# A new written-out command order, with other engines for copies and masks, in a fused attention and maxout-FFN kernel

## The chip, the cores and the metric

The kernel runs on one core of one Trainium2 chip. The metric is device time in microseconds (us). Before the change six runs gave a median of 193.53 us (192.91 to 194.72).

The core's engines work side by side, each through its own queue in order: PE (TensorE: matmuls and transposes through the array), DVE (VectorE), ACT (ScalarE), POOL (GpSimd) and SP (SyncE, which here only issues transfers). An instruction that waits holds up everything behind it on its engine; semaphores tie the engines to one another.

## The reference, cut to what matters

```python
# q, k, v: (batch 4, heads 8, seq 768, head_dim 64)
scores = scale * q @ k.T                       # per batch and head
keep   = causal                                # retrieval heads (0, 2, 6)
keep   = causal & (first 4 keys | last 64)     # streaming heads (the others)
a      = softmax(where(keep, scores, -1e9))
x      = (a @ v), heads side by side           # (3072 tokens, 512)
h      = max(x @ w1, x @ w2, x @ w3)           # (3072, 768)
out    = h @ w_out                             # (3072, 512), float32
```

## The kernel before, in words

**Tiling.** The sequence of each of the four batches is cut into two halves of 384 tokens (three blocks of 128). A step `t` of the attention is a batch, a half and one of two groups of four heads: `t = 4*batch + 2*half + group`, 16 in all, and each step is worked as two pairs of heads (`i` = 0 or 1). The FFN (line 570) is worked per half batch, so eight times; it needs the attention output of all four head pairs of that half (steps `4*batch + 2*half` and the next one).

**The order is written by hand.** The whole kernel is the list of strings `PROGRAM` (line 132). `run` (line 895) reads it from the first command to the last and calls one small function for each. The scheduler is told to keep that order (`tc.manual_schedule()`), so a command's place in the list is its place in the queue of each engine that it uses. The commands, with the line of the function:

- `ld`, `load`, `load_v`, `load_vp`, `w` (279, 350, 406, 552): transfers from HBM. `ld`, `load`, `load_vp` and `w` (the four weight matrices, converted to half precision on the way) are issued by POOL, `load_v` by SP. The first q and k are loaded ahead of the program by SP and ACT.
- `cast`, `turnp` (310, 322): for batch 0, conversion of k and q to half precision, and transposes through PE, copied out of PSUM (line 341). The last letters name the engines: `d` DVE, `a` ACT, `p` POOL; `cast 0 0 pd` casts k on POOL and q on DVE.
- `turn b g i part` (380): for batches 1 to 3, a quarter of the transposes of one group of heads, on DVE (line 388).
- `um`, `o` (531, 363): mask tables, and the copies of the first keys into places where streaming heads find them.
- `s t u [i]` (690): score matmuls of unit `u` of step `t` into the PSUM tiles `st` (two buffers, each holds one pair of heads), and their exponentials on ACT (line 748).
- `k t i u e` (754): multiplies the exponentials by 0/1 masks, on DVE or POOL, one to three instructions (lines 762, 782, 797).
- `v t i ee` (651): v to half precision (line 656, the first letter), and copies for the streaming heads (lines 660 to 672, the second letter).
- `av t i` (801): products with v into a PSUM bank, then the reciprocal of the sums and the scaling, both on DVE (lines 831, 834).
- `x t i e` (840): transposes the scaled output for the FFN. `D` is one transposing transfer issued by SP (line 847); `a` and `d` are three transposes on PE and a copy on ACT or DVE (lines 853, 854).
- `f 1 e` (641): one step of the FFN that is at the head of a queue. Of the 24 steps of one FFN, 18 are products: four matmuls of 128x384 (line 591) into a PSUM bank; a third of them are then copied out by ACT or DVE, as `e` says (line 608), the others go through a maximum on DVE always (line 611). In the first two stages (batch 0) the six products with w1 come first, then w2's, then w3's; later the three alternate. The other six are three output steps (six matmuls of 128x512, line 627, a copy by ACT or DVE at line 633, a transfer by SP at line 634), each followed by an empty one.
- `gate`, `pad` (400, 397): transfers of a few bytes on SP.

There are four PSUM banks for everything but the scores (`bkp`, line 253): products, outputs, `av` and transposes share them. A buffer that is asked for again waits for whoever still reads it: three each for v (`vs`), for the transposed q and k (`KQ`), for each xT and for the output tile (`ot`).

The idea of the order is that the FFN steps of one half batch fill PE while the other engines work on the attention of the next one. Below, "step n of the FFN stage" counts the `f` commands, 192 in all: stage 0 is f 1 to 24, stage 1 is f 25 to 48, and so on.

The four lines in which the output's transposes and the FFN meet:

```python
if op is None:                                   # D
    nc.sync.dma_start(out=xt, in_=..., transpose=True)
...
if hp == NHP - 1:
    queue.append(ffn(b, half))
```

Of the kernel before, what the change touches and what calls it, by code (L numbers as in the profile page):

```python
# [129 lines left out]
)  # L130

PROGRAM = (
    "cast 0 0 ad, load_v 0 0, cast 0 1 pp, ld 1 0, um 1 1, turnp 0 1 aa, um 1 0, cast 0 3 pa",
    "um 0 1, s 0 0 1, s 0 1 1 b, turnp 0 3 a, cast 0 2 pp, ld 1 2, turnp 0 0 ad, turnp 0 2 ad",
    "um 0 0, cast 1 1 dd, s 0 0 0, cast 1 0 dd, w 0, s 1 0 0, s 0 1 0 b, load_vp 0 1, o 0 0 0 p",
    "v 0 1 dd, v 1 1 dd, v 0 0 dp, turnp 1 0 d, turnp 1 1 da, s 1 0 1, av 0 0, w 1, av 0 1",
    "o 0 1 0 p, cast 1 2 pa, s 1 1 1, s 1 1 0 b, s 2 0 1, v 1 0 pp, cast 1 3 ap, av 1 1",
    "s 2 0 0, av 1 0, x 1 0 d, x 0 0 a, turnp 1 2 dd, s 2 1, x 0 1 d, w 2, x 1 1 d, turnp 1 3 d",
    "f 1 d, s 3 0, k 2 0 1 d, f 1 d, k 3 0 0 d, w 3, o 0 0 1 p, s 3 1 0, k 3 1 0 d, f 1 a",
    "f 1 d, o 0 1 1 d, k 2 1 1 d, s 2 2, v 3 0 dp, f 1 d, k 3 0 1 d, load 1 0, f 1 d, k 2 0 2 d",  # L140
    "v 2 1 dd, s 2 3, av 3 0, s 3 1 1, f 1 a, f 1 d, f 1 d, k 2 1 3 p, v 3 1 ap, k 2 0 3 d",
    "f 1 d, av 2 1, k 3 1 1 p, f 1 a, f 1 d, gate, f 1 d, f 1 d, v 2 0 ad, f 1 a, av 3 1, f 1 d",
    "av 2 0, f 1 a, f 1 d, load 1 1, x 2 0 a, x 3 0 a, f 1 a, load_v 1 0, load 2 0",
    "turn 1 0 0 0, f 1 d, turn 1 0 0 1, x 2 1 a, turn 1 0 1 0, x 3 1 a, f 1 a, f 1 d, f 1 a",
    "turn 1 0 1 1, turn 1 1 0 1, f 1 a, f 1 a, f 1 a, f 1 a, f 1 a, turn 1 1 0 0, f 1 a",
    "turn 1 1 1 1, f 1 a, turn 1 1 1 0, f 1 d, turn 2 0 0 0, load_v 1 1, s 5 0, k 5 0 0 p",
    "f 1 a, load 2 1, f 1 d, f 1 d, s 4 0, turn 2 0 1 1, f 1 a, k 4 0 0 d, f 1 d, f 1 d, s 5 1",
    "o 1 0 0 d, f 1 d, f 1 a, k 4 1 0 d, s 4 1, k 5 1 0 d, o 1 1 0 p, v 5 0 pp, f 1 a, s 5 2",
    "v 4 0 dp, k 4 0 1 d, f 1 a, k 4 1 1 d, k 5 0 2 d, f 1 d, av 4 0, v 4 1 pd, v 5 1 ap",
    "turn 2 0 0 1, s 6 0, f 1 a, k 5 1 2 p, av 5 0, v 6 0 dd, av 4 1, s 6 1, x 4 0 D, f 1 a",  # L150
    "k 6 0 1 p, av 5 1, turn 2 0 1 0, x 5 0 D, k 5 0 1 d, x 4 1 D, k 6 1 1 p, f 1 a, f 1 d",
    "v 7 1 pp, s 6 2, k 6 0 2 d, x 5 1 a, f 1 a, v 7 0 pp, f 1 a, s 6 3, turn 2 1 1 1",
    "turn 2 1 1 0, f 1 a, v 6 1 pd, f 1 a, k 6 1 3 p, f 1 d, turn 2 1 0 1, f 1 a, turn 2 1 0 0",
    "f 1 d, f 1 a, f 1 a, av 6 1, k 5 1 1 p, s 8 0, f 1 d, av 7 0, load_v 2 0, f 1 a, load 3 1",
    "pad, k 6 0 3 d, av 7 1, s 9 0, x 6 1 D, f 1 d, f 1 d, v 9 1 pp, f 1 a, v 9 0 dp, f 1 a",
    "v 8 1 dd, s 9 1, f 1 a, turn 3 1 1 1, av 6 0, load 3 0, o 2 0 0 d, x 6 0 D, turn 3 1 0 0",
    "f 1 a, x 7 0 D, x 7 1 D, s 8 1, f 1 a, f 1 d, s 10 0, o 2 1 0 p, f 1 d, k 8 0 1 d, f 1 a",
    "turn 3 1 1 0, load_v 2 1, s 9 2, k 9 0 2 d, k 9 1 2 d, f 1 a, f 1 a, v 8 0 ap, f 1 d",
    "f 1 a, k 8 0 0 p, k 9 0 0 d, turn 3 1 0 1, v 10 0 pd, v 11 1 pp, f 1 d, f 1 a, load_v 3 0",
    "f 1 d, f 1 d, f 1 a, k 8 1 0 d, k 9 1 0 d, s 10 1, av 9 0, f 1 a, av 8 0, f 1 a, f 1 a",  # L160
    "v 11 0 pd, f 1 d, f 1 d, k 8 1 1 d, f 1 a, v 12 0 dp, k 9 1 1 p, s 10 2, x 8 0 D, av 9 1",
    "f 1 d, f 1 a, f 1 a, s 10 3, turn 3 0 0 0, av 8 1, x 9 0 D, f 1 a, f 1 d, x 8 1 D, f 1 a",
    "f 1 d, k 10 0 1 p, f 1 d, turn 3 0 0 1, x 9 1 D, k 10 0 3 d, k 10 0 2 d, turn 3 0 1 0",
    "f 1 a, f 1 d, f 1 d, load_v 3 1, f 1 a, k 9 0 1 d, av 10 0, f 1 a, k 10 1 3 p, f 1 d",
    "f 1 d, v 12 1 pp, f 1 a, turn 3 0 1 1, av 11 0, k 10 1 1 p, f 1 d, f 1 a, f 1 a, s 13 0",
    "v 13 1 pp, f 1 d, av 11 1, f 1 d, f 1 a, x 10 0 D, x 11 0 D, v 10 1 ap, v 15 1 pd, s 12 0",
    "f 1 a, f 1 d, f 1 a, f 1 d, f 1 a, k 13 1 0 d, s 13 1, o 3 1 0 p, f 1 a, av 10 1, s 12 1",
    "k 13 0 0 d, f 1 d, f 1 a, s 14 0, k 12 1 1 p, x 10 1 D, f 1 d, x 11 1 D, f 1 a, f 1 d",
    "k 12 0 0 d, f 1 a, f 1 d, k 12 1 0 d, f 1 a, f 1 a, k 13 0 1 d, f 1 d, v 14 1 dd",
    "o 3 0 0 p, s 13 2, k 13 1 1 d, f 1 d, f 1 d, f 1 d, k 13 1 2 p, av 12 1, k 12 0 1 p",  # L170
    "s 14 1, f 1 d, f 1 a, f 1 a, f 1 a, f 1 a, k 13 0 2 d, f 1 a, f 1 d, av 13 1, s 14 2",
    "v 13 0 dp, f 1 d, av 12 0, v 15 0 ap, f 1 d, v 14 0 pp, k 14 0 2 p, f 1 d, k 14 1 1 d",
    "x 12 1 D, f 1 a, av 13 0, f 1 a, x 13 0 D, s 14 3, f 1 d, f 1 a, f 1 d, x 12 0 D, x 13 1 D",
    "f 1 d, f 1 a, f 1 a, k 14 0 3 p, f 1 d, av 15 0, f 1 d, f 1 d, k 14 0 1 d, f 1 d, av 15 1",
    "f 1 a, f 1 d, k 14 1 3 d, f 1 a, av 14 0, f 1 d, av 14 1, f 1 a, f 1 a, f 1 d, f 1 a",
    "x 14 0 D, x 14 1 D, f 1 d, f 1 d, f 1 d, f 1 a, f 1 d, f 1 a, f 1 a, f 1 d, f 1 d",
    "x 15 0 D, x 15 1 D, f 1 a, f 1 a, f 1 a, f 1 a, f 1 a, f 1 d, f 1 d, f 1 d, f 1 d, f 1 a",
    "f 1 a, f 1 d, f 1 a, f 1 a, f 1 a, f 1 d, f 1 a, f 1 d, f 1 a, f 1 a, f 1 d, f 1 a, f 1 a",
    "f 1 a, f 1 a, f 1 d, f 1 a, f 1 d, f 1 d, f 1 d",
)  # L180


# [774 lines left out]
```

## Time and profile before

| what | before |
|---|---|
| median of six runs | 193.53 us |
| the profiled execution, its own time | 193.86 us |
| its span, first to last instruction | 192.0 us |
| PE busy | 179.4 us, 93% of the span |
| DVE busy | 145.5 us, 76% |
| ACT busy | 98.6 us, 51% |
| POOL busy | 66.6 us, 35% |
| mean granted PE clock | 0.997 |
| HBM read, written | 25.17 MB, 6.29 MB |
| first FFN matmul starts at | 23.54 us |
| last matmul ends at about | 187.4 us |
| transposing transfers of outputs | 23, issued between 65.1 and 164.2 us |

All times of the profile count from the first instruction of the span. A group row reads: line, engine, operation, output and inputs, shapes, count, then busy time, the mean of one in ns, and the idle time of that engine just ahead of it with what ended that idle time. "Busy" of PE counts from the issue of a matmul to its modelled end, and these overlap, so it is more than the time that the matmuls take one after another: a product step of four 128x384 matmuls starts 0.65 us after the one ahead of it.

### The profile page before, as it was taken

What the parts mean: (1) busy time and instruction counts of PE and PEld (TensorE: products, weight loads), DVE (VectorE), ACT (ScalarE), POOL (GpSimd) and SP (SyncE); (2) the same over time, 40 slices, a digit from 0 to 9 for tenths busy, and PEclk for the clock granted to TensorE, in tenths of its full rate; (3) what the DMA queues carried; (4) which work ended last, traced back from release to release, by engine and by line L of the source; (5) the groups of instructions that cost most, each with busy time, mean ns of one, the idle gap of its engine ahead of it and who ended that gap; (6) DMA issues with size and microseconds to landing.
All of it is one profiled execution on the core that took longest, in us unless ns stands there. A gap on an engine that the chain in (4) does not pass through costs nothing.

```text
span 192.0 us, 4762 instructions
## 1 busy us (share of the span) xinstructions
PE 179.4 (93%) x1881; PEld 104.8 (55%) x1881; DVE 145.5 (76%) x312; ACT 98.6 (51%) x150; POOL 66.6 (35%) x114
## 2 busy tenths in 40 slices
PE   7697899999999999999969999999999999999990
PEld 2365545765555546664545566564665566546550
DVE  4139899999799989987997898858789577616720
ACT  3577997036777993679636325573735100131130
POOL 3795607700293788250445700030517100000000
PEclk9999999999999999999999999999999999999998
DMA  5999999999974259749982239412201422121013
GB/s 169 287 297 236 238 211 208 215 210 237 276 130 90 79 151 202 148 79 185 275 187 41 44 114 243 17 24 79 110 0 21 120 112 56 30 109 55 0 55 117
DMA packets 42101, 26.20 MB, mean 136 GB/s; under 512 B 32411, under 2 KB 37083, under 8 KB 42075
## 3 DMA queue, kind: packets, MB, share of 16 engines
q1 hardware_dynamic: 35818, 14.59, 32.2%
q0 software_dynamic: 4880, 10.23, 27.2%
q10 hardware_dynamic: 1376, 1.05, 1.7%
q8 instruction: 15, 0.25, 0.5%
q14 instruction: 12, 0.09, 0.2%
HBM read 25.17 MB, written 6.29 MB: 164 GB/s over the span
## 4 chain that ended last, share of the span: by engine, by line
PE 77%; DMA 11%; DVE 5%; ACT 2%; issue 1%; POOL 1%; SPq 0%; ACTq 0%; POOLq 0%; DVEq 0%
PE yy L591 44%; PE yy L627 13%; PE st L737 9%; PE oacc L823 7%; DMA kf<-in_q_dram 3%; DMA out_dram<-ot 3%; PE yst L591 3%; DMA ks<-in_k_dram 2%; DMA xT<-x 2%; ACT pb L748 1%; DVE KQ L341 1%; PE yst L627 1%; PE tr L853 1%; DVE pn L762 1%; DVE x L834 1%
## 5 line engine op out<-in xcount | busy, mean ns | idle before, releaser
L591 PE MATMUL yy<-xT,w0t 128*128 128x384 f16 x180 | 35.9, 327 | 1.6 <-DVE x L834 1.5
L591 PE MATMUL yy<-xT,w1t 128*128 128x384 f16 x180 | 35.6, 327 | 0.3 <-DVE acc L611 0.3
L591 PE MATMUL yy<-xT,w2t 128*128 128x384 f16 x180 | 35.9, 327 | 0.0
L748 ACT ACTIVATE pb<-st 128x1024 f16<-128x1024 f32 (+1 forms) x32 | 29.4, 972 | 7.6 <-PE st L737 7.4
L611 DVE TENSOR_TENSOR acc<-yy,acc 128x384 f16<-128x384 f32 x45 | 25.1, 558 | 9.8 <-PE yy L591 7.0
L627 PE MATMUL yy<-woutt,hT 128*128 128x512 f16 (+1 forms) x138 | 31.7, 375 | 0.0
L608 ACT CAST acc<-yy 128x384 f16<-128x384 f32 x28 | 13.5, 481 | 31.9 <-PE yy L591 26.5
L611 DVE TENSOR_TENSOR hT<-yy,acc 128x384 f16<-128x384 f32 x45 | 24.9, 556 | 3.6 <-PE yy L591 0.8
L388 DVE STREAM_TRANSPOSE KQ<-kq 128x384 f32<-128x384 f32 x24 | 25.4, 1134 | 1.2 <-PE st L737 1.2
L591 PEld LDWEIGHTS <-w0t 128*128 128x128 f16 x192 | 17.9, 98 | 15.0 <-DVE x L834 1.9
L737 PE MATMUL st<-KQ 32*128 32x128 f16 (+5 forms) x560 | 24.2, 253 | 0.9 <-POOL KQ L378 0.2
L591 PEld LDWEIGHTS <-w1t 128*128 128x128 f16 x192 | 17.8, 98 | 11.9 <-issue 0.4
L748 ACT ACTIVATE pn<-st 128x1024 f16<-128x1024 f32 (+4 forms) x27 | 22.1, 864 | 4.1 <-PE st L737 3.2
L591 PEld LDWEIGHTS <-w2t 128*128 128x128 f16 x192 | 17.6, 98 | 11.3 <-issue 0.4
L627 PEld LDWEIGHTS <-hT 128*128 128x128 f16 x150 | 14.2, 98 | 14.6 <-DVE hT L611 0.4
L737 PEld LDWEIGHTS <-KQ 32*128 32x128 f16 (+1 forms) x560 | 11.9, 93 | 13.8 <-issue 10.6
L633 ACT COPY ot<-yy 128x512 f32<-128x512 f32 x17 | 10.0, 588 | 17.4 <-PE yy L627 13.9
L834 DVE TENSOR_TENSOR x<-oacc,rc 128x384 f16<-128x384 f32 x32 | 17.8, 558 | 1.2
L762 POOL TENSOR_TENSOR pn<-pn,mk 128x512 f16<-128x512 f16 (+2 forms) x7 | 10.9, 1566 | 22.2 <-ACT pn L748 14.6
L748 ACT ACTIVATE pa<-st 128x1024 f16<-128x1024 f32 (+2 forms) x18 | 12.3, 738 | 5.8 <-PE st L737 5.8
L762 DVE TENSOR_TENSOR pn<-pn,mk 128x512 f16<-128x512 f16 (+3 forms) x23 | 13.5, 619 | 1.0 <-ACT pn L748 1.0
L656 POOL CAST va<-vs 128x384 f16<-128x384 f32 x14 | 7.7, 555 | 12.1 <-DMA vs<-in_v_dram 11.8
(96 smaller groups left out, 197.5 us busy)
## 6 DMA issues: line engine op xcount, KB each, us to landing
out_dram<-ot SPq DMA_DIRECT2D x23, 256.0 KB, 2.2
vs<-in_v_dram SPq DMA_DIRECT2D x21, 256.0 KB, 4.4
kq<-in_k_dram POOLq DMA_DIRECT2D x3, 384.0 KB, 7.4
kq<-in_q_dram POOLq DMA_DIRECT2D x3, 384.0 KB, 8.7
kq<-in_k_dram POOLq DMA_DIRECT2D x3, 288.0 KB, 4.7
kq<-in_q_dram POOLq DMA_DIRECT2D x3, 288.0 KB, 5.5
qs<-in_q_dram ACTq DMA_DIRECT2D x4, 192.0 KB, 3.9
ks<-in_k_dram SPq DMA_DIRECT2D x4, 192.0 KB, 4.8
```

What stands on the lines that cost most here:

```text
L388: nc.vector.transpose(out=dst.rearrange("c (p j) -> c j p", j=n)[:, j0:j1], in_=src.rearrange("c (j i) -> c j i", i=R),)
L591: nc.tensor.matmul(yy[:, 0:HALF], w_t[wi][:, ks, ni * P : (ni + 1) * P], xT[b, half][ks].rearrange("p a t -> p (a t)"), start=(ks == 0), s ...
L608: copy_out[0](out=acc[ni], in_=yy[:, 0:HALF])
L611: nc.vector.tensor_tensor(out=dst, in0=yy[:, 0:HALF], in1=acc[ni], op=ALU.max)
L627: nc.tensor.matmul(yo[:, 0:n], hT[ns][:, tb * P : (tb + 1) * P], woutt[:, ns, c : c + n], start=(ns == 0), stop=(ns == NNB - 1),)
L633: op(out=ot[:, c : c + n], in_=yo[:, 0:n])
L656: op(out=va[j][:, hs, k0 : k0 + HB, 0:D], in_=vs[:, hs])
L737: nc.tensor.matmul(sts[g // m][:, g % m, c0 : c0 + n * P], KQ[r0 : r0 + nr, 0, abs(ki) * P : (abs(ki) + 1) * P], KQ[r0 : r0 + nr, 1, q0 * ...
L748: nc.scalar.activation(out=pts[of_step(t, i)][:, h0 : h0 + m, off : off + w], in_=st[:, :, 0:w], func=AF.Exp, scale=sc,)
L762: engine.tensor_tensor(out=x, in0=x, in1=m.to_broadcast([P, 2, r, n]), op=ALU.mult)
L823: nc.tensor.matmul(o[:, qi, hl, 0 : D + 1], pt[:, hl, c : c + P], vv[:, 0 : D + 1], start=(idx == 0), stop=(idx == len(todo) - 1), skip_gr ...
L834: nc.vector.tensor_tensor(out=xs[b, half][:, i : i + 3 : 2, :, qd].rearrange("p h a d -> p a h d"), in0=o[:, :, :, 0:D], in1=rc.unsqueeze( ...
```

## The change

Only the strings of `PROGRAM` change; no function does. The multiset of commands stays the same but for one `pad` more (462 commands in place of 461) and for the engine letters. The order is new from the first command on.

What differs by count: of 54 `k` commands 36 name DVE and 18 POOL before, 22 and 32 after. `x ... D` goes from 23 to 22, `x ... a` from 6 to 5, `x ... d` from 3 to 5. The `v` casts (first letter) go from 12 DVE, 6 ACT, 14 POOL to 6, 9, 17. The `f` letters hardly change (102 `a` and 90 `d` before, 101 and 91 after), but they stand elsewhere.

What differs by place, as far as the prediction speaks of it (the listing is cut; a line that is only three dots marks what is left out):

```diff
-    "cast 0 0 ad, load_v 0 0, cast 0 1 pp, ld 1 0, um 1 1, turnp 0 1 aa, um 1 0, cast 0 3 pa",
-    "um 0 1, s 0 0 1, s 0 1 1 b, turnp 0 3 a, cast 0 2 pp, ld 1 2, turnp 0 0 ad, turnp 0 2 ad",
-    "um 0 0, cast 1 1 dd, s 0 0 0, cast 1 0 dd, w 0, s 1 0 0, s 0 1 0 b, load_vp 0 1, o 0 0 0 p",
-    "v 0 1 dd, v 1 1 dd, v 0 0 dp, turnp 1 0 d, turnp 1 1 da, s 1 0 1, av 0 0, w 1, av 0 1",
-    "o 0 1 0 p, cast 1 2 pa, s 1 1 1, s 1 1 0 b, s 2 0 1, v 1 0 pp, cast 1 3 ap, av 1 1",
-    "s 2 0 0, av 1 0, x 1 0 d, x 0 0 a, turnp 1 2 dd, s 2 1, x 0 1 d, w 2, x 1 1 d, turnp 1 3 d",
-    "f 1 d, s 3 0, k 2 0 1 d, f 1 d, k 3 0 0 d, w 3, o 0 0 1 p, s 3 1 0, k 3 1 0 d, f 1 a",
+    "cast 0 1 pp, ld 1 0, cast 0 0 pd, load_v 0 0, um 1 1, turnp 0 1 ad, um 0 1, cast 0 3 dp",
+    "cast 0 2 pp, s 0 0 1, um 1 0, s 0 1 1 b, turnp 0 0 dd, ld 1 2, turnp 0 3 da, s 0 0 0",
+    "um 0 0, turnp 0 2 dd, v 0 1 dd, cast 1 0 pa, s 1 0 1, w 0, turnp 1 0 ad, cast 1 1 pd",
+    "v 0 0 pp, av 0 1, s 2 0 0, o 0 1 0 p, s 1 0 0, v 1 1 pd, o 0 0 0 d, s 1 1 1, s 0 1 0 b",
+    "cast 1 2 pa, cast 1 3 da, turnp 1 1 dd, s 1 1 0 b, av 1 1, s 2 0 1, av 0 0, load_vp 0 1",
+    "turnp 1 2 aa, v 1 0 pp, av 1 0, s 2 1, x 0 1 d, turnp 1 3 d, x 0 0 d, x 1 0 d, x 1 1 d",
+    "s 3 0, w 1, o 0 0 1 p, k 3 0 0 d, f 1 d, k 2 0 1 d, f 1 d, s 2 2, v 3 0 dd, w 2, w 3",
...
-    "turn 1 0 0 0, f 1 d, turn 1 0 0 1, x 2 1 a, turn 1 0 1 0, x 3 1 a, f 1 a, f 1 d, f 1 a",
-    "turn 1 0 1 1, turn 1 1 0 1, f 1 a, f 1 a, f 1 a, f 1 a, f 1 a, turn 1 1 0 0, f 1 a",
+    "x 3 1 a, load_v 1 0, turn 1 0 0 0, f 1 a, load 1 1, f 1 a, turn 1 0 1 0, f 1 a",
+    "turn 1 0 1 1, f 1 a, turn 1 1 0 0, f 1 a, f 1 a, turn 1 1 0 1, turn 1 1 1 0, load 2 0",
...
-    "k 6 0 1 p, av 5 1, turn 2 0 1 0, x 5 0 D, k 5 0 1 d, x 4 1 D, k 6 1 1 p, f 1 a, f 1 d",
-    "v 7 1 pp, s 6 2, k 6 0 2 d, x 5 1 a, f 1 a, v 7 0 pp, f 1 a, s 6 3, turn 2 1 1 1",
+    "x 4 1 D, x 5 0 a, f 1 a, f 1 d, turn 2 0 0 1, load_v 2 1, turn 2 0 1 0, f 1 a, k 6 1 1 p",
+    "s 6 2, x 5 1 d, f 1 a, s 6 3, turn 2 1 0 0, f 1 d, f 1 a, turn 2 1 1 0, v 7 0 pp, f 1 d",
...
-    "turn 3 1 1 0, load_v 2 1, s 9 2, k 9 0 2 d, k 9 1 2 d, f 1 a, f 1 a, v 8 0 ap, f 1 d",
-    "f 1 a, k 8 0 0 p, k 9 0 0 d, turn 3 1 0 1, v 10 0 pd, v 11 1 pp, f 1 d, f 1 a, load_v 3 0",
-    "f 1 d, f 1 d, f 1 a, k 8 1 0 d, k 9 1 0 d, s 10 1, av 9 0, f 1 a, av 8 0, f 1 a, f 1 a",
+    "v 8 0 ap, f 1 a, f 1 d, k 8 0 0 d, v 11 0 pp, v 8 1 dp, s 9 2, k 8 1 1 d, f 1 d",
+    "load_v 3 0, f 1 d, k 9 0 2 p, av 8 0, turn 3 1 1 0, f 1 a, load 3 0, f 1 d, f 1 a",
+    "k 9 1 2 d, s 10 1, k 8 1 0 p, f 1 d, f 1 a, f 1 a, f 1 a, v 12 0 pp, av 9 0, f 1 d",
...
-    "x 12 1 D, f 1 a, av 13 0, f 1 a, x 13 0 D, s 14 3, f 1 d, f 1 a, f 1 d, x 12 0 D, x 13 1 D",
+    "v 15 1 dd, f 1 a, f 1 a, x 13 0 D, f 1 a, f 1 d, s 14 2, k 14 0 1 p, x 12 1 D, k 14 0 2 p",
+    "av 15 0, x 13 1 D, f 1 d, f 1 a, f 1 a, f 1 d, f 1 d, f 1 a, k 14 1 1 p, f 1 d, f 1 a",
...
```

## The prediction

> **What bounds the kernel now.** I read the page first, then busy time by FFN stage, then what PE waited for, then the places of those waits in the timeline.
>
> ```profile
> PE 179.4 (93%) x1881; PEld 104.8 (55%) x1881; DVE 145.5 (76%) x312; ACT 98.6 (51%) x150; POOL 66.6 (35%) x114
> ```
>
> PE is the bound. The table of stretches, cut at the first FFN matmul and at each stage's first one, shows where it is not full (columns: stretch, its length, then busy us of PE, weight loads, DVE, ACT, POOL):
>
> ```profile
> 0.00:23.50 23.50, 17.98 (x180) 10.54 (x181) 13.11 (x46) 15.15 (x27) 15.82 (x33) 1.00 1.02 246
> 23.50:45.30 21.80, 21.56 (x220) 12.83 (x218) 20.59 (x45) 11.49 (x19) 7.19 (x13) 1.00 1.13 214
> 45.30:69.90 24.60, 24.25 (x299) 13.40 (x298) 22.61 (x44) 19.65 (x28) 13.74 (x21) 1.00 0.65 146
> 69.90:91.80 21.90, 21.90 (x290) 13.05 (x289) 19.24 (x36) 15.44 (x23) 9.43 (x18) 1.00 0.88 166
> 91.80:113.60 21.80, 19.93 (x199) 11.40 (x198) 20.07 (x40) 9.61 (x15) 10.68 (x16) 1.00 0.55 125
> ```
>
> PE idles in the lead-in and in the stage from 91.8 (1.87 us); later stages have at most 0.1. DVE is the second bound: 92% of the stage from 45.3. The waits of PE, and the place of the largest:
>
> ```profile
> PE yy L591 <- DVE x L834: 1.5, 1, 1.5
> PE yy L591 <- DVE acc L611: 0.3, 1, 0.3
> ```
> ```profile
> 91.25 3.17 DVE L762 TENSOR_TENSOR pn<-pn,mk 128x1024 f16<-128x1024 f16 x3 [0.22 <-ACT pn L748]
> 92.36 1.77 POOL L797 TENSOR_TENSOR pa<-pa,mk 128x512 f16<-128x512 f16 x2
> 97.13 1.37 DVE L762 TENSOR_TENSOR pn<-pn,mk 128x512 f16<-128x512 f16 x2
> 99.25 0.82 PE L591 MATMUL yy<-xT,w0t 128*128 128x384 f16 x4 [1.51 <-DVE x L834]
> ```
>
> DVE runs five masks of group 1 around 91 to 98 with a `turn` between, reaches the FFN's maxima late, and PE runs out of PSUM banks. The transfers that the change reckons anew show only once, in the chain that ended last:
>
> ```profile
> 150.35 4.13 DMA xT<-x
> ```
>
> There the first product of the next stage takes 1.08 us for its four matmuls (start 153.77) where others take 0.81: 0.27 us lost. So at most 1.87 + 0.27 = 2.1 us of the steady part can be won, and whatever the lead-in gives.
>
> **The sum.** It is made against the profiled execution, 193.86 us, a span of 192.0 and 1.86 around it; I take the difference over to the median, 193.53, which lies 0.33 lower. PE's work is fixed: 192 FFN steps, 43 score commands, 32 `av`. Costs not named stay beside PE.
>
> *One more transpose on PE.* Ten `x` on PE instead of nine: 3 transposes, half of the 0.34 between the starts of a group of six and what follows: +0.17, certain.
>
> *The stall at 96 to 99.* In the new list the masks there are spread: k 9 0 0, 9 1 0 and 9 0 2 (0.92, 0.92, 0.69 on DVE) go to POOL, k 9 1 1 (0.6) comes back. For f 73 to 96 I price every command by its row: DVE 18.0 before (the trace has 20.07, with the slowed masks in it), 16.5 after, of which masks 3.3 and 1.3. Walking DVE from f 67 on (turn 1.0, k 8 0 0 0.76, v 0.36, k 8 1 1 0.30, copy 0.69, av 0.75, turn 1.0, four maxima 0.55 each, k 9 1 2 0.69) I find it about 1 us behind PE, and four banks cover 4 x 0.65 = 2.6. Gain between 0 and 1.87; I take 1.6.
>
> *The xT wait.* x 12 0, 13 0, 12 1, 13 1 come at f 132 to 137 instead of 133 to 138. Four issues of 1.2 us and 2.3 to landing then end some 2 us ahead of f 145. Gain 0.27 (ends 0 and 0.27). The other stages have their transposes 6 to 9 steps ahead in both lists; x 14 and 15 too (f 153 to 161 for f 169).
>
> *The lead-in.* Before, f 1 starts at 23.54 and s 3 0 follows; f 2 starts at 25.11. After, s 3 0 stands ahead of f 1, and ACT, which feeds it, has its queue set anew. These rows show the chain before:
>
> ```profile
> 17.30 1.02 ACT L748 ACTIVATE pn<-st 128x1024 f16<-128x1024 f32 x1 [0.29 <-PE st L737]
> 22.75 1.94 ACT L748 ACTIVATE pb<-st 128x1024 f16<-128x1024 f32 x2 [0.19 <-PE st L737]
> 24.72 2.43 ACT L748 ACTIVATE pn<-st 128x1024 f16<-128x1024 f32 x3
> ```
>
> In the new list cast 1 0's q stands on ACT ahead of s 1 0 1. Its data, the second transfer of ld 1 0, landed at 14.2 (7.89 + 6.30 in the chain), and POOL reaches ld 1 0 at the same time as before. Queued behind the wait are, to the end of s 2 1: the cast 0.5; eight exponentials of 128x1024 or their like (s 1 0 1, s 2 0 0, s 1 0 0, s 2 0 1, s 2 1 twice: 6 x 1.0; s 1 1 1 0.33, s 0 1 0 0.66, s 1 1 0 0.5); copies of turnp 1 0 and 1 2, 3 x 0.48; two casts 1.0. That is 10.4, plus about 0.4 of waits for PE: 14.25 + 10.8 = 25.0. s 3 0's second pair needs the PSUM tile that s 2 1's last exponential frees, so f 1 starts at 25.0 to 25.3 where before one FFN step more was done at 25.11: +0.55 to +0.85. If ACT closes up (starts overlap by some 0.07), s 3 0 costs nothing: -0.2. If POOL is late too (load_vp, 2.72 of issuing, now stands straight ahead of v 1 0, whose `av` feeds x 1 0): +1.5. I take +0.7. The weights are covered: w 0 is issued 2 us later (11.48 before, landed 8.7 later at 20.2, used 23.5), w 1 some 3.4 later (landed 27.5, used 30.9), but transfers of that queue landed one after another every 3.5 to 4 us, so all move by less than 2. If that cover is gone: up to +1 more. v 3 0, now whole on DVE, waits for load_vp, with DVE's k 2 1 1 and copies of f 4 and f 5 behind it, and PE's av 3 0 waits for k 3 0 1 of that queue: +0.2 (0 to 1.5).
>
> *Stage 1 (f 25 to 48).* Here DVE gets more. Priced the same way its work is 22.5 before (the trace has 22.61) and 25.7 after: nine `turn` instead of seven (+2.0), two copies more for FFN steps (+1.2), x 5 1 (+0.36), v (-0.3). PE's 24.6 grows by 0.7 (one more score command in the stage). So DVE has 25.7 for 25.3 of PE. Eight turns in a row (0.97 each) end when s 5 0 needs them; x 5 1's copy stands behind turn 2 0 0 1 and 2 0 1 0, and f 49 needs it; s 8 0 needs turn 2 1 0 1, which I find done 0.2 us ahead of it. Ends: 0 if the banks take the lag up, +2.5 if each of the three costs. Such a lag gave 1.87 in the stage from 91.8. I take +1.0.
>
> *Masks and casts that go to POOL.* Nineteen `k` go to POOL and five come back; in instructions 48 on DVE and 20 on POOL become 28 and 40. A mask of 128x512 takes 0.40 to 0.65 on DVE, 1.15 on POOL. In sum DVE's masks fall from 21.8 to 13.1, POOL's rise from 23.5 to 45.1, and POOL's total from 66 to 87 of 192. Their results are due late: k 6 0 1 ends at about 78.3 and av 6 0 comes at 81.5; k 13 0 2 at 135.3, av 13 0 at 138.1. If POOL ran 3 us later than I reckon, those margins would be gone, +0.5 each. But DVE pays:
>
> ```profile
> L762 DVE TENSOR_TENSOR pn<-pn,mk x23: 285/548/2226, 26.4 to 141.6; 128x512 f16<-128x512 f16 x11, 128x768 f16<-128x768 f16 x6, 128x1024 f16<-128x1024 f16 x4, 128x256 f16<-128x256 f16 x2
> L611 DVE TENSOR_TENSOR acc<-yy,acc x45: 536/558/596, 31.8 to 181.0; 128x384 f16<-128x384 f32 x45
> ```
>
> The 2226 ns mask stands at 92.2, beside POOL's two masks (alone, at 141.56, that size takes 0.68). [...] The maxima (one input from PSUM) show no such thing: 536 to 596 ns. By the rows taken alone the move frees DVE of 8.6 us. [...]
>
> Together: 0.17 - 1.6 - 0.27 + 0.7 + 0.2 + 1.0 = +0.2. **Predicted 193.7 us.** PE's switches between kinds of work are as many, and clock and tail are as before.
>
> **The rivals.** *Faster, 191.8:* the freed DVE is all that counts; the stage from 91.8 loses its whole wait, the xT wait goes, the lead-in is level: 193.53 - 1.87 - 0.27 + 0.17 + 0.2. For it: DVE caused the only large wait. Against: DVE gets more where it was at 92%.
>
> *Slower, 196.0:* stage 1. DVE, with nine turns, falls more than 2.6 us (four banks) behind PE between f 30 and f 57; from that point each us of lag is a us of PE. Price: 2.5 there, and 0.7 of the lead-in, less 0.6 of the old stall (contention with POOL's fuller queue in stage 2 keeps it half alive): about +2.5. For it: 25.7 against 25.3. Against: DVE idled 2.0 us in that stage before, and lags fade in stage 2 (19.8 after, 22.5 before).
>
> *Lead-in, 194.9:* ACT and POOL late together, +1.5 before f 1; stage 1 loses what the old stall gives; -0.27 and +0.17 as above.
>
> *The change doesn't do what it says:* the transposing transfers cost 0.27 in all, so timing them better gives nothing, and the new order differs by chance alone. That is near my forecast.
>
> **How the numbers follow.** Near level, 193.7 (own range 192.6 to 194.5): 0.37. Faster: 0.25. Stage 1: 0.26; lead-in: 0.12. What a measurement of this kernel can tell from no change is about 0.5%, 0.97 us: under 192.56 is faster, over 194.50 slower. Of the cases this gives 0.25, 0.37, 0.38. The range reaches from 191.4 (the faster case with a level lead-in a little early) to 196.3 (stage 1 at its upper end).
>
> **What would show it.** Right: f 1 starts at 24.8 to 25.4, with one s more ahead of it; no PE wait over 0.5 in the stage after f 73; DVE busy over 25 in stage 1; the first product of stage 6 in 0.81. Wrong: f 1 at or ahead of 23.6 (ACT not the limit); PE waits of 1 us or more for DVE in stage 1 (the slower rival); PE waiting for POOL masks ahead of `av` 6 0 or 13 0, which I hold to be covered by some 3 us; a weight landing after its first use; SP held by load_v 3 1 or 3 0 with an output transfer behind it.

## The result and the profile after

The kernel after takes 192.44 us in the median of 19 runs (191.03 to 193.70), the kernel before beside it 193.72. The ratio of the runs is 0.9925, with a 95% interval of 0.9903 to 0.9948: faster by 0.75%. The profiled execution after took 192.51, with a span of 190.8 (before 193.86 and 192.0). The page and the table of stretches, in the columns of the ones shown before (behind POOL's stand the granted clock of PE, the DMA share and GB/s):

```profile
PE 178.7 (94%) x1884; PEld 104.7 (55%) x1884; DVE 142.3 (75%) x303; ACT 94.1 (49%) x143; POOL 88.1 (46%) x133
```
```profile
45.70:69.90 24.20, 24.03 (x302) 13.37 (x300) 22.27 (x44) 18.96 (x27) 11.64 (x20) 1.00 0.74 169
69.90:92.00 22.10, 22.10 (x303) 13.40 (x302) 18.74 (x37) 16.01 (x25) 17.02 (x27) 1.00 0.92 196
92.00:110.40 18.40, 18.40 (x167) 10.43 (x164) 16.17 (x30) 8.76 (x13) 11.06 (x14) 1.00 0.73 139
110.40:131.50 21.10, 21.10 (x274) 12.52 (x273) 15.25 (x31) 10.35 (x14) 12.18 (x17) 1.00 0.20 57
```

The stage from 92 is 18.4 us long instead of 21.8, with PE full; POOL works 11.1 us in it and DVE only 16.2. The stage from 45.7, for which I feared, has DVE at 22.3, hardly less than before, and is no longer. The first FFN matmul of each stage, and the last matmul's end, in the two traces:

| | st. 0 | 1 | 2 | 3 | 4 | 5 | 6 | 7 | last matmul ends | span ends |
|---|---|---|---|---|---|---|---|---|---|---|
| before | 23.54 | 45.33 | 69.88 | 91.80 | 113.60 | 134.56 | 153.77 | 171.68 | 187.44 | 192.04 |
| after | 24.62 | 45.68 | 69.89 | 91.99 | 110.45 | 131.50 | 150.94 | 169.14 | 184.90 | 190.79 |
| after less before | +1.08 | +0.35 | 0.0 | +0.2 | -3.15 | -3.06 | -2.83 | -2.54 | -2.54 | -1.25 |

The whole gain comes in one stage, and of the 2.54 us that are left of it at the last matmul, half are lost behind that. (Stage 3 has the same 18.46 in the traces of e10 and e12 below, which keep this order there.) The granted clock of PE was 0.50 from 8.77 to 15.59 us in the trace of after, and in that of before, as far as it has the clock (from 13.38), 1.00. That is not what set the first FFN matmul: e12, at 1.00 from 13.45 on, starts it at 24.75, and e2, with such a stretch from 7.73 to 14.56, at 23.53. Where PE waited before for `yy`, nothing is left. This is the stretch in which POOL has its big mask now; DVE beside it copies out of PSUM, scales and transposes:

```profile
91.59 2.12 POOL L762 TENSOR_TENSOR pn<-pn,mk 128x1024 f16<-128x1024 f16 x1 [0.18 <-ACT pn L748]
91.82 0.69 DVE L633 COPY ot<-yy 128x512 f32<-128x512 f32 x1 [1.52 <-PE yy L627]
92.64 0.56 DVE L834 TENSOR_TENSOR x<-oacc,rc 128x384 f16<-128x384 f32 x1
93.12 1.12 DVE L388 STREAM_TRANSPOSE KQ<-kq 128x384 f32<-128x384 f32 x1
```

All three take what they take in the whole kernel after (means of 0.69, 0.56 and 1.14 us for these shapes). Before, a mask of DVE stood there and took 2.2 us. It was one of 128x512, which takes 0.42 by itself, as the row of line 762 in that stretch of before shows: the two of 128x1024 are the middle ones, at 0.69, so those of 128x512 took 420 and 2226 ns.

```profile
L762 DVE TENSOR_TENSOR pn<-pn,mk x4: 420/693/2226, 90.3 to 92.2; 128x1024 f16<-128x1024 f16 x2, 128x512 f16<-128x512 f16 x2
```

The group row of DVE's masks has a longest of 836 ns for the whole kernel after, where it was 2226:

```profile
L762 DVE TENSOR_TENSOR pn<-pn,mk x15: 285/549/836, 25.2 to 150.5; 128x768 f16<-128x768 f16 x6, 128x512 f16<-128x512 f16 x4, 128x1024 f16<-128x1024 f16 x3, 128x256 f16<-128x256 f16 x2
```

The lead-in, and the wait of PE just ahead of the first FFN step that the new order brings (`s 3 0`'s second pair, as foreseen):

```profile
24.28 0.40 PE L737 MATMUL st<-KQ 64*128 64x128 f16 x8 [0.52 <-ACT pb L748]
24.62 1.47 PE L591 MATMUL yy<-xT,w0t 128*128 128x384 f16 x8
```

The end. PE's last branch in the view of line 922 (ns: shortest, median, longest), first before, then after, and what SP waited for there after (us in all, times, longest; before it was 2.3, 4, 0.9):

```profile
L922 PEldq COMPARE_BRANCH  x1: 379/379/379, 185.0 to 185.0; - x1
```
```profile
L922 PEldq COMPARE_BRANCH  x1: 3101/3101/3101, 182.6 to 182.6; - x1
```
```profile
SPq L922 <- SPq L922: 3.6, 4, 2.3
```

PE's branch over the part of the program that isn't taken (line 922) lasts 3.1 us instead of 0.4, and SP sees the last output transfer land 3.7 us after its issue (185.4 to 189.1) instead of 2.4 (187.9 to 190.3). The page counts 16 packets in the instruction queue where before there were 15 (each has 16,384 bytes in the traces' lists of DMA packets), and that list has the extra one at 186.45 to 187.90: the last output's packets stop at 187.38 and go on at 187.90.

### The profile page after: what moved, and what is told of

Its sections match the earlier page's. It is cut to its first block, busy times and chain, and to the rows that moved or that the text cites. A ratio compares the mean times of both kernels' runs of the same rounds, so it can differ in the third digit from the quotient of the medians.

```text
span 190.8 us, 4772 instructions
## 1 busy us (share of the span) xinstructions
PE 178.7 (94%) x1884; PEld 104.7 (55%) x1884; DVE 142.3 (75%) x303; ACT 94.1 (49%) x143; POOL 88.1 (46%) x133
## 4 chain that ended last, share of the span: by engine, by line
PE 85%; DMA 6%; ACT 3%; SPq 1%; DVE 1%; issue 0%; DVEq 0%; ACTq 0%
PE yy L591 47%; PE yy L627 16%; PE st L737 9%; PE oacc L823 8%; DMA vs<-in_v_dram 5%; PE yst L591 3%; ACT pb L748 2%; DMA qs<-in_q_dram 1%; PE yst L627 1%; SPq L412 0%; PE st L722 0%; ACT KQ L341 0%; ACT ot L633 0%; DVE KQ L341 0%; SPq L916 0%
## 5 line engine op out<-in xcount | busy, mean ns | idle before, releaser
L591 PE MATMUL yy<-xT,w2t 128*128 128x384 f16 x180 | 35.4, 327 | 0.0
L762 POOL TENSOR_TENSOR pn<-pn,mk 128x512 f16<-128x512 f16 (+2 forms) x15 | 20.9, 1417 | 20.4 <-ACT pn L748 16.0
L608 ACT CAST acc<-yy 128x384 f16<-128x384 f32 x26 | 12.5, 479 | 35.4 <-PE yy L591 32.0
L737 PE MATMUL st<-KQ 32*128 32x128 f16 (+4 forms) x560 | 23.9, 253 | 1.1 <-ACT pb L748 0.5
L633 ACT COPY ot<-yy 128x512 f32<-128x512 f32 x14 | 8.3, 589 | 21.0 <-PE yy L627 18.4
L797 POOL TENSOR_TENSOR pb<-pb,mk 128x512 f16<-128x512 f16 x10 | 11.4, 1152 | 11.9 <-ACT pb L748 11.8
L633 DVE COPY ot<-yy 128x512 f32<-128x512 f32 (+1 forms) x9 | 6.0, 662 | 11.5 <-PE yy L627 10.9
## 6 DMA issues: line engine op xcount, KB each, us to landing
qs<-in_q_dram ACTq DMA_DIRECT2D x4, 192.0 KB, 5.9
ks<-in_k_dram SPq DMA_DIRECT2D x4, 192.0 KB, 4.7
```

What stands on the lines that cost most here:

```text
L591: nc.tensor.matmul(yy[:, 0:HALF], w_t[wi][:, ks, ni * P : (ni + 1) * P], xT[b, half][ks].rearrange("p a t -> p (a t)"), start=(ks == 0), s ...
L608: copy_out[0](out=acc[ni], in_=yy[:, 0:HALF])
L633: op(out=ot[:, c : c + n], in_=yo[:, 0:n])
L737: nc.tensor.matmul(sts[g // m][:, g % m, c0 : c0 + n * P], KQ[r0 : r0 + nr, 0, abs(ki) * P : (abs(ki) + 1) * P], KQ[r0 : r0 + nr, 1, q0 * ...
L762: engine.tensor_tensor(out=x, in0=x, in1=m.to_broadcast([P, 2, r, n]), op=ALU.mult)
L797: engine.tensor_tensor(out=x, in0=x, in1=m, op=ALU.mult)
```

## The experiments

Each kernel ran beside the kernel before on the same chip. The medians of before there were 193.75 to 194.05, so the ratios are what is compared.

| run | what differs | median | ratio to before, 95% |
|---|---|---|---|
| e1 | old order, three masks to POOL, one back | 194.96 | 1.0028 (0.9999 to 1.0057) |
| e2 | old order, all new mask letters | 195.28 | 1.0077 (1.0050 to 1.0103) |
| e3 | new order, all old mask letters | 199.40 | 1.0234 (1.0182 to 1.0286) |
| e4 | new, x 5 0 as transposing transfer | 192.68 | 0.9930 (0.9909 to 0.9952) |
| e5 | old, k 8 0 0 to DVE | 191.65 | 0.9889 (0.9848 to 0.9930) |
| e6 | as e5, two casts from POOL to ACT | 195.93 | 1.0109 (1.0057 to 1.0162) |
| e7 | old up to f 60, then new | 193.95 | 1.0025 (1.0000 to 1.0051) |
| e8 | new up to f 60, then old | 196.56 | 1.0140 (1.0086 to 1.0194) |
| e9 | old, k 8 0 0 on POOL but earlier | 192.60 | 0.9927 (0.9901 to 0.9953) |
| e10 | new, one warm-up matmul fewer | 191.57 | 0.9879 (0.9835 to 0.9922) |
| e11 | e5 with four warm-ups more | 193.10 | 0.9942 (0.9916 to 0.9969) |
| e12 | new, k 8 0 0 back to POOL | 192.69 | 0.9923 (0.9893 to 0.9953) |

**e1: the three masks of my prediction, alone.** My theory at first (M) was that of the prediction: DVE had too many masks around 91 to 98. (The slow one of before is the second mask of k 9 0 0, one of the three.)

```diff
-"... k 9 0 2 d, ..."  "... k 9 0 0 d, ..."  "... k 9 1 0 d, ..."  "... k 9 1 1 p, ..."
+"... k 9 0 2 p, ..."  "... k 9 0 0 p, ..."  "... k 9 1 0 p, ..."  "... k 9 1 1 d, ..."
```

> The order of before, and every engine letter of before but four: k 9 0 0, k 9 1 0 and k 9 0 2 go to POOL, k 9 1 1 comes back to DVE, as in the kernel after. Theory M (the masks around 91 to 98 us put DVE late, and that is the whole stall): PE's 1.5 us wait at 97.7 goes or shrinks under 0.3, the stage from 91.8 shortens from 21.8 to about 20.2, and the time falls by about 1.6, to 192.1. Theory O (the order as a whole, the places of turns, scores and FFN steps, made the stage shorter; the letters matter little): the wait stays over 1 us, time 193.3 to 193.8. A third, theory P (the masks on POOL slow DVE's masks beside them, or are themselves late for av 9): the wait moves to av 9 0 or 9 1, 194 or more.

Measured: no gain at all; theory P. The stage from 91.6 is 21.75 long. Its wait has moved, and other masks of DVE are now slow (PE's waits, and lines of the timeline):

```profile
PE oacc L823 <- POOL pn L762: 1.9, 2, 1.0
```
```profile
90.27 2.12 POOL L762 TENSOR_TENSOR pn<-pn,mk 128x1024 f16<-128x1024 f16 x1 [5.95 <-ACT pn L748]
...
91.06 1.87 DVE L762 TENSOR_TENSOR pn<-pn,mk 128x1024 f16<-128x1024 f16 x1 [1.66 <-ACT pn L748]
...
94.73 1.14 POOL L762 TENSOR_TENSOR pn<-pn,mk 128x512 f16<-128x512 f16 x1
...
94.94 3.09 DVE L782 TENSOR_TENSOR pa<-pa,base 128x256 f16<-128x256 f16 x1
```

The mask of 128x1024 that starts at 91.06 under POOL's ends 0.5 us after POOL's does, 1.87 long instead of 0.68. The one of 128x256, 0.28 elsewhere, takes 3.09: POOL has two masks of 1.15 and two casts there with no gap between them, and DVE's mask ends at 98.03, 0.14 us after the second cast. Less work on DVE freed no time on DVE: it is busy 20.2 us from 91.6 to 113.4, where it was 20.1 in that stage of before. The traced execution, 193.52, is the fastest of this kernel's 22 runs; what the median of 194.96 pays more is in no trace, but goes with the granted clock (see e6).

**e2 and e3: letters without the order, order without the letters.** The 24 letters of `k` commands that the change turned, in the other kernel's order (the letters of `v`, `x`, `cast` and `f` stay with the order); two of the 24 here, first for e2, then for e3:

```diff
-k 2 0 2 d, ... k 3 1 1 p
+k 2 0 2 p, ... k 3 1 1 d
...
-k 3 1 1 d, ... k 2 0 2 p
+k 3 1 1 p, ... k 2 0 2 d
```

> The order of before, with the mask engines of the kernel after for all 54 k commands (19 to POOL, 5 back to DVE). Theory M: stage from 91.8 loses its wait, no other stage gains one, 191.9 to 192.3. Theory O: 193.3 to 193.8, the wait at 97.7 over 1 us. Theory P: POOL, with masks at places that the old order did not make ready, is late for av 6 or av 13, PE waits for it, 194 to 195.

> The order of after, with the mask engines of the kernel before for all 54 k commands. Theory M: DVE gets its 8.6 us of masks back, a wait of 1 to 2 us for a maximum or an av copy returns in the stage from 92.0, time about 194.0. Theory O: stages as in the kernel after (18.4 for the stage from 92.0), 192.2 to 192.7.

Measured: 0.8% slower and 2.3% slower, where both together are 0.75% faster. Theory O falls with e3, M with e2. In e2, k 8 0 0 is on DVE, the one letter of e5 below; but its 128x512 mask stands beside two masks of k 9 0 0, now POOL's, and takes 2.67 us. In e3 three stages are long (stretches from the first FFN matmul of stage 1, 2, 3 on):

```profile
46.30:72.70 26.40, 24.34 (x301) 13.39 (x299) 23.91 (x43) 18.92 (x27) 15.19 (x22) 1.00 0.67 154
72.70:96.60 23.90, 22.80 (x303) 13.52 (x302) 23.21 (x41) 16.39 (x26) 9.14 (x19) 1.00 0.82 180
96.60:117.10 20.50, 19.13 (x167) 10.40 (x164) 18.95 (x35) 8.58 (x13) 9.94 (x16) 1.00 0.59 124
```

DVE is busy 156.0 us in it, 13.7 more than after, though the masks that came back are 8.6 by the rows (the prediction's figure). Against the undisturbed durations of their shapes, DVE's masks take 9.7 us too long in e3, 1.5 in the kernel after and 4.0 in that of before. Of the 9.7, 9.5 fall on masks that stand beside POOL's work.

**e4: the tail.** Theory F came from the two traces' ends.

```diff
-"x 4 1 D, x 5 0 a, f 1 a, ..."
+"x 4 1 D, x 5 0 D, f 1 a, ..."
```

> The kernel after with x 5 0 as a transposing transfer (D) as before: PE has 6 instructions fewer, as many as before, nothing else differs. Theory F (a 16 KB block of PE's code is fetched at the very end of the kernel after because of where the end of PE's code falls, and its DMA packet of 1.45 us stands ahead of the last output's packets): with PE's code ending where it did before, the last output lands 2.0 us after its issue instead of 3.3, the span loses 1.3 and the time is 191.0 or less with a smaller spread. Theory N (the longer tail is chance of that one execution): the same spread as the kernel after, median 192.2 to 192.5; the transpose saved is worth 0.17.

Measured: the branch is back at 0.38 and the second fetch gone, and the last output is seen 2.9 us after its issue instead of 3.7. But the time is that of the kernel after (0.9930 against 0.9925). SP issues the four transfers of stage 2 from 85.1 on instead of 83.2, the last one lands late, and PE waits in the midst of a product:

```profile
93.37 0.32 PE L591 MATMUL yy<-xT,w0t 128*128 128x384 f16 x1 [0.70 <-DMA xT<-x]
```

That transfer was issued at 89.5; its first parts landed 2.2 later, its last one 3.8 later, and a packet of instructions ran from 91.2 to 92.3. Whether the one transfer more set SP back is not shown: e12, which has no transfer more, issues its four from 84.3. So a saving at the tail met a price elsewhere, and e4 could not decide on F's size.

**e5: one letter.** By now I held theory C: the stall of before was a collision between masks on the two engines, not an amount of work. Only a test that gives DVE more to do can tell these apart.

```diff
-"f 1 a, k 8 0 0 p, k 9 0 0 d, turn 3 1 0 1, ..."
+"f 1 a, k 8 0 0 d, k 9 0 0 d, turn 3 1 0 1, ..."
```

> The kernel before with one letter changed: k 8 0 0 (two masks of 128x512 beside which the 2226 ns mask of DVE stood at 92.2) goes from POOL to DVE, so that DVE has more to do in the very stretch where it was late. Theory C (the stall is a collision: a DVE mask slows two to three times while POOL works on SBUF beside it; the amount of DVE work is not the cause): the slow mask falls from 2.2 to 0.7, DVE pays 0.8 for the new ones, so DVE gains some 0.7, PE's waits in the stage from 91.8 fall from 1.87 to about 1.1, time 193.2 against 194.0. Theory M (amount): DVE has 0.8 more, the waits grow to about 2.6, time 194.8.

Measured: 1.1% faster, C's direction and more than its size. The stretch of DVE, and the stage:

```profile
91.02 0.69 DVE L762 TENSOR_TENSOR pn<-pn,mk 128x1024 f16<-128x1024 f16 x1 [0.22 <-ACT pn L748]
91.62 0.68 DVE L797 TENSOR_TENSOR pa<-pa,mk 128x512 f16<-128x512 f16 x2
92.23 0.75 DVE L762 TENSOR_TENSOR pn<-pn,mk 128x512 f16<-128x512 f16 x2
```
```profile
91.60:111.20 19.60, 19.60 (x199) 11.30 (x198) 17.87 (x41) 9.59 (x15) 8.75 (x14) 1.00 0.60 138
```

DVE has two masks more, and its `turn` starts 1.3 us after the stage's first matmul (92.90) instead of 2.5 (94.34). PE has no wait left in that stage. I had reckoned with 0.7 of gain; it was 2.1: PE's gaps in the stage went from 2.4 us to 0.25. Two things were missing in the 0.7. The slow mask lost 1.8 us, not 1.5, since it is one of 128x512. And DVE, earlier by then, does its next masks ahead of POOL's casts of v (from 96.06); before, three of these masks stood beside such casts (96.62 to 98.50) and lost another 0.9. The last matmul ends at 184.81, as early as in the kernel after (184.90).

**e6: quieter still.**

```diff
-"... v 10 0 pd, v 11 1 pp, ..."
+"... v 10 0 ad, v 11 1 ap, ..."
```

> As the run before it, and the casts v 10 0 and v 11 1, which POOL worked on beside DVE's 1.37 us pair of masks at 97, go to ACT, which was idle for 3 us there. Theory C: the pair falls from 1.37 to 0.80 too, PE's waits in the stage fall to about 0.6, time 192.8 to 193.0. Theory M: no gain over the run before it, 194.8; or ACT's casts stand ahead of an exponential and cost a wait of PE for st, 195.

Measured: 1.1% slower than before, for a reason that I had named only as an aside. The casts wait 3.8 us for a transfer of v that lands at 96.9, and the copy of an FFN bank that stands behind them in ACT's queue starts at 97.72 (ACT's timeline, PE's wait, and a stretch of the table):

```profile
96.89 0.92 ACT L656 CAST va<-vs 128x384 f16<-128x384 f32 x2 [3.80 <-DMA vs<-in_v_dram]
```
```profile
PE oacc L823 <- ACT acc L608: 2.6, 1, 2.6
```
```profile
99.20:102.60 3.40, 3.40 (x23) 1.75 (x22) 3.33 (x11) 1.22 (x2) 0.00 (x0) 0.50 0.31 65
```

On POOL the same wait (3.9 us in e5) had nobody behind it for whom PE waited. More than PE's 2.6 us is lost: 0.9 us after that wait's end the granted clock of PE goes to 0.50 for 3.4 us, in which product matmuls start 0.32 apart instead of 0.16. So the stage is 24.05 long, 4.4 more than in e5. In e8 the same follows two waits of 1.1 and 1.4 us that lie close together (0.50 from 96.38 to 99.79). In the stage from 91.8 of before, with its waits of 0.35 and 1.5, the clock stays at 1.00. What brings such a stretch on is not shown.

This bears on e1's spread too. One such stretch lowers the mean granted clock of a run by 0.009 (half of 3.4 us, of 194). Of e1's runs, the four at 0.997 or more took 193.5 to 193.7 us and the six at 0.991 took 194.9 to 195.6. That PE's waits in the latter were followed by such a stretch is likely, but not shown: no trace of them is there.

**e7 and e8: crossing the orders over at f 60.** Each takes one list up to step f 60 and then the other's commands that are still undone, in its order and with its letters. The seam of e7, against before:

```diff
 "f 1 d, f 1 d, v 9 1 pp, f 1 a, v 9 0 dp, ...
-f 1 a, v 8 1 dd, s 9 1, f 1 a, turn 3 1 1 1, av 6 0, ...
+load_v 2 1, load_v 3 1, f 1 a, turn 3 1 0 1, k 9 0 0 p, av 6 0, s 9 1, ...
```

> Commands and letters of before up to step f 60, then all the rest in the order and with the letters of after (462 commands; x 5 0 stays a transposing transfer, so PE has as many instructions as before). Theory S (the gain sits in the stage from 92 alone; lead-in and the first stages give nothing): stages up to f 60 as before, the stage from f 73 about 18.4 to 19.3, last work 2.5 earlier than before, and by theory F no code fetch on top of the last output, so 191.2 to 191.8. Rival, theory W (the early part of the new order, its turns and masks of group 2 and 3 done sooner, is what the later part lives from): the later part finds masks and scores undone at f 60, 193.5 or more.

> The mirror: commands and letters of after up to f 60, then the rest of before (PE's instruction count is that of after). Theory S: the stage from f 73 has the old stall and length, 21.8, and the tail is 1.3 longer, as in the kernel after: 194.5 to 195.3. Theory W: half of the gain or more is there, 192.5 to 193.

Measured: 0.25% and 1.4% slower. Theory S falls in its strict form: the new second half alone doesn't bring the gain. e7's 193.95 is the number that W gave, but not for W's reason. In e7 the stage from 92.2 is 20.1 long and has no late mask, but one transfer (lines are one lower, this list has a string less):

```profile
PE yy L590 <- DMA xT<-x: 1.4, 1, 1.4
```

That one is issued at 90.1, after two loads of v that the seam put ahead, and it lands at 94.2; after, it is issued at 87.1 and lands at 89.4. In e8 such waits are 2.5 us (those transfers take up to 7.8 us from issue to landing), and the old collision is there too, and the stretch at half the clock. A list joined of two halves has troubles of its own, so these two say little of where the gain sits; they do show what a late transfer costs.

**e9: the same letters, the mask earlier.** e5 changes an engine and a moment at once. This changes the moment alone.

```diff
-"... f 1 a, f 1 a, v 8 0 ap, f 1 d",  "f 1 a, k 8 0 0 p, k 9 0 0 d, ..."
+"... f 1 a, f 1 a, k 8 0 0 p, v 8 0 ap, f 1 d",  "f 1 a, k 9 0 0 d, ..."
```

> The kernel before with every letter as it was; only k 8 0 0 p stands ahead of v 8 0 ap instead of some commands behind it, so that POOL does the same two masks at about 86 to 88, where it was idle and DVE works on the FFN's maxima, instead of at 92.4 beside DVE's masks. Theory C (collision): the same gain as from the letter, the 2226 ns mask takes 0.7, no PE wait over 0.5 in the stage from 91.8, 191.5 to 192.0. Theory L (it was POOL's slowness, the lateness of its result for av 8 0, that the letter took away): av 8 0 gets its masks sooner too, but DVE's mask is slowed wherever POOL works; gain at most half, 192.7 to 193.7.

Measured: 0.73% faster with the same work on the same engines. The time, 192.60, lies between C's range and L's; the trace decides. The stage from 92.6 is 19.6 long, as in e5. But 0.85 us was paid in the stage ahead of it, where POOL's two masks now stand beside another copy of DVE's within SBUF, which takes 1.24 there instead of 0.35 (e5, at 84.96):

```profile
84.36 1.77 POOL L797 TENSOR_TENSOR pa<-pa,mk 128x512 f16<-128x512 f16 x2
...
85.11 1.24 DVE L378 COPY KQ<-KQ 32x32 f16<-32x32 f16 x2
```

PE then waits 0.7 for an `hT` in that stage. So C holds for the cause, and what L said of slowing DVE wherever POOL works is true of that copy. L's own cause, POOL's late result for av 8 0, is not among PE's waits in that stage of before: these are for DVE's lines 834 and 611.

**e10 and e11: the tail by itself.** The edit is the number of matmuls of zeros at the start (line 72), which moves the end of PE's code and nothing in the steady part.

```diff
-IDLE = 8
+IDLE = 7        (e10; in e11, on the kernel of e5: 12)
```

> The kernel after with seven instead of eight matmuls of zeros at the start (line 72), so that PE's code is two instructions shorter (3781 in place of 3783 in the trace's count; the kernels with 3781 and fewer had no second 16 KB fetch at the end, those with 3782 and 3783 had it). Theory F: PE's last branch takes 0.38 instead of 3.1, no fetch lies on the last output, the span ends 4.5 to 5.2 after the last matmul instead of 5.9, median 191.2 to 191.7. Theory N: the tail is as long, median 192.3 to 192.5.

> The mirror of that on the fast variant of the old order (k 8 0 0 on DVE, 191.65): twelve instead of eight matmuls of zeros, 1.7 us of PE at the start where it is idle for 5.8, so that PE has 3783 instructions. Theory F: the long branch and the second fetch appear, the last output lands 1.3 later, 192.6 to 193.0. Theory N: 191.6 to 191.8. If the warm-ups themselves cost, the first FFN matmul starts later than 23.4 and that is to be taken off.

Measured: e10 as F had it, 191.57, the fastest kernel of this study by its median. Its stages have the lengths of the kernel after, to 0.05 us; the end differs:

```profile
L922 PEldq COMPARE_BRANCH  x1: 379/379/379, 182.3 to 182.3; - x1
```
```profile
SPq L922 <- SPq L922: 2.4, 5, 0.7
```

e11 has the long branch and the second fetch, as foretold, 193.10 in the median against e5's 191.65. Of that, 0.9 stands in the lead-in (first FFN matmul at 24.20 instead of 23.33). Whether the warm-ups are to blame is open: e6, with eight of them, has 24.06. In e11's trace the fetch, at 187.7, met the last output less badly (seen 2.6 after its issue). So the fetch follows the length of PE's code: the traces with 3782 PE instructions and more (after, e3, e11, e12) have it, those with 3781 and fewer (the other ten) don't. From the last matmul to the end it is 5.9 us in after and e3, which have the fetch, 4.8 and 4.9 in e11 and e12, which have it too, and 4.5 to 5.1 in the ten without. So its price is up to 1.3, where it meets the last packets, and in e11 and e12 it can't be told from none.

**e12: the same letter in the new order.**

```diff
-"v 8 0 ap, f 1 a, f 1 d, k 8 0 0 d, v 11 0 pp, ..."
+"v 8 0 ap, f 1 a, f 1 d, k 8 0 0 p, v 11 0 pp, ..."
```

> The kernel after with the same single letter turned the other way: k 8 0 0 from DVE back to POOL, as before the change. Theory C: what it costs depends on what DVE does beside it; POOL has it at about 89 to 91 here, ahead of the masks at 91.6, which move 2.3 later, beside DVE's mask at 95.2: that one slows by about 1, with little PE wait since DVE has room there: 192.4 to 193.2. Theory A (the amount on DVE, or the letter alone, is the whole difference of the kernels): 194.0 to 194.5.

Measured: as the kernel after (0.9923 against 0.9925). The letter that is worth 1.1% in the old order is worth nothing here, since in the new one no mask of DVE stands beside it. Theory A falls. C's own guess, that a later mask of DVE would be slowed by about 1 us, didn't come true either: it takes 0.68.

**The collision over all runs.** For each trace I took what DVE's masks and v casts that start between 92 and 112 us took beyond the same shape's undisturbed time, and PE's gaps over its usual spacing in that stage, without stretches at half the clock (both to 0.1 or 0.2 us):

| | before | e1 | e2 | e3 | e8 | after | e5 | e9 | e12 |
|---|---|---|---|---|---|---|---|---|---|
| DVE's masks slowed by, us | 2.8 | 2.9 | 2.3 | 4.1 | 2.7 | 0.2 | 0.1 | 0.2 | 0.0 |
| PE's gaps in the stage, us | 2.4 | 2.5 | 2.8 | 2.3 | 2.7 | 0.25 | 0.25 | 0.25 | 0.25 |

In e1 and e2 a mask that starts just ahead of 92 is slowed by another 1.2 and 1.1. e6 and e7 have no slowed masks (0.1 and 0.2) and gaps of 3.1 and 1.9, of the other causes told above.

## Why the prediction was wrong

I forecast level, 193.7, and put a quarter on faster; it was faster by 1.3 us, which is beyond the interval of the ratio. The time lies in my whole range (191.4 to 196.3), but just outside the one for level (192.6 to 194.5). It is nearer to the faster rival's 191.8, whose reason (the freed DVE) is not the right one. The step that failed is stage 1: I held DVE to be the bound there and added 1.0 us; the stage became 0.34 shorter. With the stage as measured (-0.34, the transpose's 0.17 included) the sum would have come to -1.3, close to the measured -1.25, but by luck, for two other steps were wrong and cancel in part. Up to the start of stage 2 I forecast +2.07 and the traces have 0.0; from there to the last matmul -1.87 and -2.54; behind it nothing and +1.29. By its own steps:

*One more transpose on PE, +0.17.* Right: three matmuls more, 0.056 each, in the stage from 45.7.

*The stall, -1.6.* Right in direction, wrong in cause, too small in size. I laid it to five masks of DVE in a row and reckoned DVE still 1 us behind after the change. I also misread the 2226 ns mask: it is one of 128x512 (0.42 alone), not of the size that took 0.68 at 141.56. e1 moved just the masks that I named and gained nothing; e5 gave DVE more and gained all. The stall was one mask of DVE's beside two of POOL's (1.8 us lost), and then three beside POOL's casts (0.9). In the stage from 92, 2.2 us of gaps go. It is shorter by another 1.1 because 36 `av` matmuls (0.03 each) stand in the stages before and behind it now; that part is moved, not won.

*The xT wait, -0.27.* Right: the first product of stage 6 takes 0.81, and the last of its four transfers landed 2.1 us ahead (148.8 for 150.9), where before it landed 0.7 behind the stage's start. More time for these transfers is worth a quarter of a us here. e4 and e7 show what it guards against: 0.7 and 1.4.

*The lead-in, +0.7.* Too large: f 1 starts at 24.62, not 25.0 to 25.3, and f 2 at 25.27 against 25.11. ACT's chain from the awaited cast on took 10.2 us, not 10.8: its starts overlap by about 0.1 each. What was lost, +0.35 at the next stage, is gone at 69.9.

*v 3 0, +0.2.* Nothing of it shows.

*Stage 1, +1.0.* This is the step that failed most. I priced commands by their place between the `f` commands, found nine `turn` against seven and 25.7 us on DVE, and took DVE for the bound. The trace has 22.3 us and eight `turn`, as before has eight: the queue of DVE is not cut where PE's is. Of my nine, the first begins at 45.0, ahead of the stage, and the last runs at 70.0, behind it. PE has no wait at all there and the stage became 0.34 shorter. But e3 shows that the danger was real: with the old mask letters the same order loses 2.2 us in that stage, so the moved masks pay for it there. In e3 DVE is busy 23.9 us there, 1.6 more than after, and its masks, casts and small copies lose 3.2 against their undisturbed durations (after: 0.8): the collisions alone are more than the difference.

*Masks and casts that go to POOL, no term of their own in the sum.* What DVE lost beside POOL did not grow with POOL's work: POOL was busy 66.6 us before and 88.1 after, and DVE's masks lost 4.0 us over the whole kernel before and 1.5 after. It comes in lumps. With POOL at work beside them, DVE's maxima and scalings from PSUM took 1.02 and 1.00 times their undisturbed duration and the transposes of line 388 1.01 times, masks of fp16 1.8 to 2.5 times; so what counts is which pair meets. In e1 the first slow mask ends 0.5 us after POOL's. The second, 3.09 us long, ends 0.14 after the last of four POOL instructions. The trace of before has the same picture: the mask of 2.2 us ends at 94.42, 0.3 after POOL's two (94.13), so it alone could have pointed to the cause; e5 and e9 part the masks in two ways, and each takes 2.1 or 2.2 off the stage.

*Tail as before.* Wrong by 1.3 us in the traced execution, half of what the rest had won. The order changed PE's code by eight instructions in the trace's count, to 3783, and a 16th packet of instructions was fetched at the end, as in all four traces with 3782 and more.

In sum, as measured: +0.35 to stage 1, -0.15 to stage 3, -3.35 in stage 3, +0.6 behind it (moved `av` and scores), +1.3 in the tail: -1.25 in the span. What stays open: why runs of one kernel spread by 1 to 3 us; e5's six lie within 0.9, e1's 22 within 3.4, and the traces show one execution each. In e1 much of it goes with the granted clock; in the kernel after it does not (191.4 and 192.5 at 0.979, 192.8 and 193.7 at 0.997). And e5 and e10 can't be told apart, nor surely from the kernel after, by their intervals.

## What to carry to other kernels

Before moving work from VectorE to GpSimd, or back, look at what stands beside it in the other engine's timeline: a VectorE mask of 0.42 us took 0.41 with GpSimd idle (e5) and 2.2 beside GpSimd masks (before), and one command moved was worth as much as the whole new order. An instruction that takes several times its usual duration is a cause to be followed up before any amount of work is blamed. Look also at what follows a wait: in e6 one of 2.6 us was followed by 3.4 us at half the granted clock. And when the last matmul ends 2.5 us sooner but the span only 1.25, the tail has a cause of its own; look for it in the packets behind the last output.

## What the hardware showed

*Which VectorE instructions suffer.* Over the 14 traces, with more than half of the instruction beside a GpSimd computation, the mean duration as a multiple of the same shape's undisturbed one (the shortest tenth of those beside no GpSimd work): fp16 masks 1.8 (line 762, 45 of them), 1.9 (797, 47) and 2.5 (782, 16; at most 11), v casts 1.5, the small copies of line 378 2.1. Maxima with one input from PSUM (438): 1.02, the same as alone. Transposes of line 388 (128): 1.01. Scaling from PSUM (156): 1.00. It goes both ways: POOL's copy of line 672, 0.23 us before, took 0.69 in e1 (at 92.34) and in e2 (at 92.83), each beside a mask of DVE.

*Transfers behind code fetches.* A packet of instructions (16,384 bytes in before and after) takes 0.9 to 1.5 us (one, in e2, 1.9). Where one ran ahead of a transposing transfer's last part, that landed 3.8 to 4.1 us after its issue instead of 2.3 (before, at 150.35, with the packet from 152.17 to 153.42; e4, at 89.5; e7, at 90.1), each about 1 us after the packet's end. In the four traces with a 16th packet PE's branch takes 3.1 us (after, e3) or 3.6 (e11, e12), in before, e4, e7, e8 and e10 0.38. No wait of PE for such a packet is seen in the steady part, but PE waited 0.27 to 1.4 us for these three transfers that landed behind one.
